# Keys transposed by a DMA, F and E turned first, and a fourth bank for the last block of an attention and MLP-mixer kernel

## The chip, the cores and the metric

One Trainium2 chip, one of its cores. The metric is the device time of one execution in microseconds (us), as the median of several runs.

## The reference

```python
# B=8 batches, H=8 heads, S=1024 positions, D=64 per head, all float32
k_proj = np.einsum('ks,bhsd->bhkd', E, k)        # E, F: 64 x 1024
v_proj = np.einsum('ks,bhsd->bhkd', F, v)
attn = softmax(np.matmul(q, k_proj.transpose(0, 1, 3, 2)) / 8)
x = np.matmul(attn, v_proj)                      # heads merged: B x 1024 x 512
u = x + (relu(x.T @ w_tok1) @ w_tok2).T          # token mixing, 256 wide, per batch
out = u + relu(u @ w_ch1) @ w_ch2                # channel mixing, 1536 wide
```

## The kernel before

TensorE does nearly everything. The channel mixing of a batch is done as two blocks (16 blocks in all). Each half of it is a two-by-two block product that takes seven products in place of eight, with sums and differences made by VectorE before and after. While blocks of batch b run, attention and token mixing of batch b+1 are woven in. A small list scheduler in Python decides the order of every engine's instructions ahead of time: each job has a due time (`prio`), and that order is then fixed in the program. In the traces an engine whose next instruction has to wait stands idle.

In the profile, L383 is the warm-up matmul on a zero tile, L411 the turning of E and F, L461 and L464 the projections E·k and F·v, L498 the small transposing matmuls of the projected keys, L803 the first half of a block, L898 its second half (`down_block`). In the kernel after, the same lines are L385, L413, L464 and L467, L513, L819 and L920; L575 is the matmul of the scores there (L559 before), L598 that of the attention with the projected values, whose result VectorE scales at L615 (`x_sb`), and L689 forms sums S from the transposed u (L673 before). The parts that the change touches:

```python
# the start
nc.vector.memset(vb, 0.0); nc.vector.memset(kT, 0.0)   # ... then, further down:
nc.vector.memset(zero, 0.0)                            # operand of the warm-up matmuls
for n, (src, dst) in enumerate(((EF[0], ET_sb), (EF[1], FT_sb))):   # E, then F
    ...                                                # 8 PE transposes each, one copy

# projected keys and values of a batch (batches 2 to 7: all 8 heads at once)
def kv_proj(b, h0, hn, due):
    ...                                # E k into rows 0-63 of a bank, F v into 64-127
    e = [copy -> kp[:, hs, 0, :], copy -> kp[:, hs, 1, :],       # keys twice
         copy -> vb[KP:, hs, 1, 0:D], copy -> vb[0:KP, hs, 0, 0:D]]   # 4 copies on ACT

def k_transpose(h0, hn, due):
    def mm():
        for h in range(hn):            # one 64-column matmul per head
            nc.tensor.matmul(view()[:, h, :], kp[:, h0 + h]..., ident[:KP, :KP], ...)
    ...                                # two ACT copies: the halves to the diagonal of kT

# the second half of a block: seven products, three banks
X_OF = {1: "x", 2: "x", 6: "y", 5: "y", 3: "y", 7: "z", 4: "z"}
def down_block(j):
    product(1, 0)
    act(... copy(out=view("y"), in_=view("x")) ...)     # y starts as a copy of product 1
    product(7, 1)
    product(6, 2)
    add_u(db, "db", "y", 1, 0)                          # db = y + u   (DVE)
    product(2, 3)
    add_u(o_of(0, 0), o_key(0, 0), "x", 0, 0)           # out00 = x + u
    product(5, 4)                                       # adds into y: must wait for db
    ... da = y + u ; out11 = z + da
    product(3, 5)                                       # adds into y: must wait for da
    add_u(o_of(0, 1), o_key(0, 1), "y", 0, 1)           # out01 = y + u
    store(0)                                            # 512 KB
    product(4, 6)
    ... out10 = z + db
    store(1)                                            # 512 KB
```

q and u are transposed by DMA, from the queue of SyncE (SP). Loads go out from POOL. The two "take turns" by explicit waits: k and v of batch b are loaded after the first transpose of u of batch b−2, the second transpose of u waits for the last of those loads, and the load of q waits for that transpose in turn.

The softmax here doesn't subtract the row's maximum and nothing guards it: scores larger than these inputs give would overflow.

## Time and profile before

| | before |
|---|---|
| time, median of 3 runs | 431.66 us (431.65 to 431.86) |
| profiled span | 429.8 us |
| TensorE busy | 97% of the span |
| first matmul, first projection of keys | 2.89 us, 9.94 us |
| first matmul of the last block, last matmul's start | 413.98 us, 425.13 us |

The page of the kernel before, its head: the span, each engine's busy time with its share and its number of instructions, the busy tenths of TensorE and of the DMA engines in 40 slices, and the engines' shares of the chain that ended last.

```profile
span 429.8 us, 9229 instructions
PE 415.9 (97%) x3727; PEld 336.2 (78%) x3756; DVE 321.9 (75%) x794; ACT 231.1 (54%) x428; POOL 66.3 (15%) x104
...
PE   7899999999999999999999999999999999999994
...
DMA  9999999996999785796939897498822303151122
...
PE 86%; DMA 6%; DVE 4%; ACT 2%; issue 1%; DVEq 0%
```

TensorE has work nearly all the time, in all slices but the first two and the last. So a gain has to come from matmuls that go away or from waits between them. The DMA engines are busy in the first half of the span, and have room in the second.

The four largest waits of TensorE of the kernel before from 1 to 73 us, each with whom it waited for, the total, how many and the longest:

```profile
PE ps L383 <- DVE zero L378: 2.9, 1, 2.9
PE ps L559 <- ACT kT L513: 0.9, 2, 0.6
PE ps L744 <- ACT uT L750: 0.4, 1, 0.4
PE ps L803 <- DVE S L673: 0.4, 1, 0.4
```

The first matmul waits 2.9 us for the zero tile.

The timeline of TensorE of the kernel before round one group of key transpositions (start, us, then engine, line, operation, shape, count):

```profile
176.16 0.60 PE L803 MATMUL ps<-S,wT 128*128 128x256 bf16 x4
176.69 0.41 PE L498 MATMUL ps<-ident,kp 64*128 64x64 bf16 x8
177.03 0.61 PE L803 MATMUL ps<-S,wT 128*128 128x256 bf16 x4
```

Ends of matmuls are modelled, so starts are what counts. Four matmuls of 256 columns take four slots of 0.109 us, up to 176.60; the next matmul after the group starts at 177.03. The group of eight costs PE 0.43 us, and there are six such groups in batches 2 to 7: 2.6 us.

The timeline of the last block of the kernel before (in brackets the idle time before a group and what ended it):

```profile
413.98 1.47 PE L898 MATMUL ps<-wc_sb,G 128*128 128x256 bf16 x12
...
419.63 0.68 DVE L931 TENSOR_TENSOR db<-ps,u 128x512 f32<-128x512 f32 x1
420.37 1.47 PE L898 MATMUL ps<-wc_sb,G 128*128 128x256 bf16 x12 [0.78 <-DVE db L931]
421.88 0.69 DVE L947 TENSOR_TENSOR da<-ps,u 128x512 f32<-128x512 f32 x1 [1.56 <-PE ps L898]
...
422.62 1.47 PE L898 MATMUL ps<-wc_sb,G 128*128 128x256 bf16 x12 [0.78 <-DVE da L947]
423.93 1.47 PE L898 MATMUL ps<-wT,G 128*128 128x256 bf16 x12
...
425.44 0.69 DVE L959 TENSOR_TENSOR o<-ps,db 128x512 f32<-128x512 f32 x1 [0.62 <-PE ps L898]
```

Products 5 (420.37) and 3 (422.62) each wait for VectorE to have read bank y. In every other block PE has other work to fill that time with; in the last there is none. By starts each wait costs 0.95 us. The Trainium skill ("PSUM — Partial Sum Buffer", the summary of rules for kernel authors) asks for just such a guard, by bank, and advises to read from a different bank than the one that matmuls write. The trace agrees with the cost side of it: the guard is seen as these two waits.

### The profile page before, as it was taken

To read this page: it belongs to the slowest core of one execution; us is meant where nothing else is said; L and a number is where in the kernel's file an instruction comes from. 1 tells how busy PE (TensorE), PEld (TensorE's weight loads), DVE (VectorE), ACT (ScalarE), POOL (GpSimd) and SP (SyncE) were. 2 spreads that over 40 slices of the span, in tenths; PEclk is the share of its full clock that TensorE was granted. 3 is DMA by queue.
4 is the path that set the end of the run, shared out by engine and by line. 5 is a ranking of instruction groups with operands and counts; after the bars stand their busy time and mean duration, and the time that the engine had idled before them with its cause. 6 is when DMAs were issued, how large, how long until landed. Compare 5 with 4: busy or idle time off the path is not lost.

```text
span 429.8 us, 9229 instructions
## 1 busy us (share of the span) xinstructions
PE 415.9 (97%) x3727; PEld 336.2 (78%) x3756; DVE 321.9 (75%) x794; ACT 231.1 (54%) x428; POOL 66.3 (15%) x104
## 2 busy tenths in 40 slices
PE   7899999999999999999999999999999999999994
PEld 3587886787878777787778878788778878888883
DVE  2369968797867878589577978679686887978573
ACT  1958895465457543863447644665438643444520
POOL 8443221030121110301111100211100000000000
PEclk9999999999999999999999999999999999999999
DMA  9999999996999785796939897498822303151122
GB/s 170 207 200 206 206 207 175 202 158 139 168 159 235 122 200 99 123 220 100 197 55 184 175 168 157 71 233 137 196 52 66 83 28 99 23 148 49 50 99 98
DMA packets 89513, 60.88 MB, mean 142 GB/s; under 512 B 55680, under 2 KB 84864, under 8 KB 89472
## 3 DMA queue, kind: packets, MB, share of 16 engines
q0 software_dynamic: 34944, 45.09, 53.2%
q1 hardware_dynamic: 54448, 14.95, 19.6%
q8 instruction: 29, 0.48, 0.4%
q10 hardware_dynamic: 80, 0.26, 0.3%
q14 instruction: 12, 0.10, 0.1%
HBM read 59.24 MB, written 16.78 MB: 177 GB/s over the span
## 4 chain that ended last, share of the span: by engine, by line
PE 86%; DMA 6%; DVE 4%; ACT 2%; issue 1%; DVEq 0%
PE ps L898 31%; PE ps L803 31%; PE ps L613 6%; PE ps L633 4%; DMA v_sb<-in_v_dram 3%; PE ps L582 3%; DMA uT<-u 3%; PE ps L461 3%; PE ps L559 3%; PE ps L383 1%; DVE u L644 1%; PE ps L691 1%; PE ps L718 1%; PE ps L543 1%; ACT qT L551 1%
## 5 line engine op out<-in xcount | busy, mean ns | idle before, releaser
L898 PEld LDWEIGHTS <-G 128*128 128x128 bf16 x1344 | 129.9, 98 | 25.1 <-issue 2.8
L898 PE MATMUL ps<-wc_sb,G 128*128 128x256 bf16 x768 | 104.1, 273 | 2.3 <-DVE da L947 1.5
L825 ACT ACTIVATE G<-ps 128x512 bf16<-128x512 f32 x96 | 56.7, 597 | 63.0 <-PE ps L803 62.8
L803 PEld LDWEIGHTS <-wc_sb 128*128 128x128 bf16 x768 | 73.2, 98 | 16.3 <-issue 2.4
L898 PE MATMUL ps<-wT,G 128*128 128x256 bf16 x576 | 78.2, 273 | 0.0
L803 PEld LDWEIGHTS <-wT 128*128 128x128 bf16 x576 | 55.2, 98 | 12.3 <-issue 1.2
L803 PE MATMUL ps<-S,wc_sb 128*128 128x256 bf16 x384 | 57.7, 273 | 0.3
L803 PE MATMUL ps<-uT,wc_sb 128*128 128x256 bf16 x384 | 57.8, 273 | 0.1
L803 PE MATMUL ps<-S,wT 128*128 128x256 bf16 x384 | 55.7, 273 | 0.4 <-DVE S L673 0.4
L784 DVE CUSTOM_DVE_ANT_0 g<-ps,ub 128x512 bf16<-128x512 f32 x48 | 32.8, 682 | 29.3 <-PE ps L803 29.3
L599 DVE TENSOR_TENSOR x_sb<-ps,rdn 128x256 bf16<-128x256 f32 x128 | 50.7, 415 | 0.9
L568 ACT ACTIVATE a<-ps 128x512 bf16<-128x512 f32 x64 | 37.8, 600 | 17.9 <-PE ps L559 17.2
L925 POOL DMA_DIRECT2D out_dram<-o x30 | 16.4, 545 | 192.8 <-DVE o L931 130.8
L831 ACT COPY ua<-ps 128x512 f32<-128x512 f32 x48 | 28.2, 587 | 32.9 <-PE ps L803 32.5
L644 DVE TENSOR_TENSOR u<-ps,x_sb 128x512 bf16<-128x512 f32 x56 | 37.6, 684 | 9.5 <-PE ps L633 5.4
L838 DVE TENSOR_TENSOR G<-G 128x512 bf16<-128x512 bf16 x96 | 39.8, 417 | 2.5
L784 DVE CUSTOM_DVE_ANT_0 G<-ps,ua 128x512 bf16<-128x512 f32 x48 | 32.8, 683 | 8.2 <-ACT ua L831 7.7
L844 ACT COPY ps<-ps 128x512 f32<-128x512 f32 x48 | 27.7, 577 | 17.1 <-DVE o L931 7.6
L831 ACT COPY ub<-ps 128x512 f32<-128x512 f32 x48 | 28.1, 586 | 13.6 <-PE ps L803 13.5
L594 DVE RECIPROCAL rdn<-ps 128x4 f32<-128x4 f32 x128 | 20.7, 173 | 18.0 <-PE ps L582 14.4
L582 PE MATMUL ps<-vb,a 128*128 128x130 bf16 x256 | 31.5, 220 | 0.4 <-DVE x_sb L599 0.3
L633 PE MATMUL ps<-hT_sb,wt_sb 128*128 128x512 bf16 x99 | 29.9, 379 | 0.4
(68 smaller groups left out, 496.2 us busy)
## 6 DMA issues: line engine op xcount, KB each, us to landing
out_dram<-o POOLq DMA_DIRECT2D x30, 512.0 KB, 5.6
k_sb<-in_k_dram POOLq DMA_DIRECT2D x14, 512.0 KB, 7.4
v_sb<-in_v_dram POOLq DMA_DIRECT2D x14, 512.0 KB, 11.8
q_sb<-in_q_dram POOLq DMA_DIRECT2D x14, 512.0 KB, 8.3
wc_sb<-in_moe_w_ch_dram POOLq DMA_DIRECT2D x6, 256.0 KB, 12.5
wc_sb<-in_moe_w_ch_dram POOLq DMA_DIRECT2D x4, 384.0 KB, 12.6
k_sb<-in_k_dram POOLq DMA_DIRECT2D x4, 256.0 KB, 6.8
v_sb<-in_v_dram POOLq DMA_DIRECT2D x4, 256.0 KB, 7.3
```

The source lines that it names most:

```text
L568: lambda: nc.scalar.activation(out=a_t[h % 4], in_=bank(bk), func=ACT.Exp, scale=scale),
L582: nc.tensor.matmul(view()[:, 2 * jj : 2 * jj + 2].rearrange("p c d -> p (c d)"), a_t[h % 4][:, j * P : (j + 1) * P], vb[:, h].rearrange("k ...
L599: lambda: nc.vector.tensor_tensor(out=x_sb[:, 4 * half : 4 * half + 4, h * D : (h + 1) * D], in0=view()[:, :, 0:D], in1=rdn[:, :, None].to ...
L633: nc.tensor.matmul(bank(bk), wt2_sb[:, t, si::NSI], hT_sb[:, t, :], start=(t == 0), stop=(t == TC - 1),)
L644: lambda: nc.vector.tensor_add(out=u_t[b % 2][:, si, :], in0=bank(bk), in1=x_sb[:, si, :]),
L784: nc.vector._custom_dve(TENSOR_ADD_SAT, out=out, in0=in0, in1=in1, s0=FMAX, s1=0.0)
L803: nc.tensor.matmul(t[:, c, :], w1_of(n, dd, 2 * m + c), a_of(j, n, dd), start=(n in (1, 7) and c == 0 and dd == 0), stop=(c == 1 and dd == 1),
L825: lambda: nc.scalar.activation(out=G[:, n, cs], in_=view(src), func=ACT.Relu),
L831: 512, lambda: nc.scalar.copy(out=dst, in_=view("y")), writes=[(name, s % 2)],
L838: 512, lambda: f(out=G[:, n, cs], in0=in0, in1=in1), ps=False, reads=deps,
L844: 512, lambda: nc.scalar.copy(out=view("y"), in_=view("x")), takes=[bk["y"]],
L898: nc.tensor.matmul(view(X_OF[n])[:, t, :], G[:, G_OF[n], cc, t * P : (t + 1) * P], w2_of(n, cc), start=(n in (1, 7) and t == 0 and cc == 0 ...
```

## The change

Three independent parts, each meant to take something off TensorE's path:

1. The start: the zero tile is written first, F is turned before E, and fewer warm-up matmuls are put ahead of the turning, so PE begins earlier.
2. The keys of batches 2 to 7: the projection puts the keys as blocks on the diagonal of a tile `kb`, and a single DMA transposes `kb` to `kT`. Eight small matmuls and two ACT copies per batch go. The projection is asked for 12 us earlier (`EARLY`), so that the DMA has time to land.
3. The last block: products 5 and 3 go to a fourth bank w, y is left at product 1 plus 6, and VectorE puts the two together, with eight adds in the block in place of six. The order of products is fixed as 1, 7, 6, 5, 2, 3, 4, and the output goes out in four stores of 256 KB in place of two of 512 KB.

```diff
+EARLY = 12.0
@@ the start
+    zero = tile_of([P, P], BF16, "zero")
+    nc.vector.memset(zero, 0.0)
     nc.vector.memset(vb, 0.0)
     nc.vector.memset(kT, 0.0)
+    nc.vector.memset(kb, 0.0)
...
-    zero = tile_of([P, P], BF16, "zero")
-    nc.vector.memset(zero, 0.0)
...
-    for n, (src, dst) in enumerate(((EF[0], ET_sb), (EF[1], FT_sb))):
+    for n, (src, dst) in enumerate(((EF[1], FT_sb), (EF[0], ET_sb))):
...
-            for _ in range(int((j.start - idle - 0.3) / 0.216) if spare is not None else 0):
+            for _ in range(int((j.start - idle - 0.3) / 0.216) if spare is not None and j.prio > -100 else 0):
                 blank(spare)
@@ the keys
+        if block:
+            k_to = [kb[i * KP : (i + 1) * KP, hs, i, :] for i in range(2)]
+        else:
+            k_to = [kp[:, hk, i, :] for i in range(2)]
...
+    def k_transpose_dma():
+        sp(
+            2.5,
+            lambda: nc.sync.dma_start_transpose(
+                out=kT.rearrange("p h c k -> p h (c k)"), in_=kb.rearrange("p h r d -> p (h r d)")
             ),
...
-            unit(1.9 * hn / H, lambda t, i=i: kv_proj(b, i * hn, hn, t))
-            unit(0.9 * hn / H, lambda t, i=i: k_transpose(i * hn, hn, t))
+            if b == 1:
+                unit(1.9 * hn / H, lambda t, i=i: kv_proj(b, i * hn, hn, t))
+                unit(0.9 * hn / H, lambda t, i=i: k_transpose(i * hn, hn, t))
+            else:
+                unit(1.9, lambda t: kv_proj(b, 0, H, t - EARLY, True))
+                unit(0.0, lambda t: k_transpose_dma())
@@ the last block
+        last = j == NSB - 1
+        where, opens = X_OF, (1, 7)
+        if last:
+            bk["w"] = Bank("F")
+            where, opens = {**X_OF, 5: "w", 3: "w"}, (1, 7, 5)
...
+        p5 = product(5, 3)
+        follow(p5[0], p6[1])
+        add_u(da, "da", "y", 1, 1)
+        da_w = add(da, "da", "w", da, "da")
+        follow(product(2, 4)[0], p5[1])
+        c22 = add(o_of(1, 1), o_key(1, 1), "z", da, "da")
+        store(1, (1,))
+        follow(add_u(dc, ("ub", 0), "y", 0, 1), da_w)
+        follow(add_u(db, "db", "y", 1, 0), c22)
+        follow(add_u(o_of(0, 0), o_key(0, 0), "x", 0, 0), c22)
+        product(3, 5)
+        store(0, (0,))
+        add(o_of(0, 1), o_key(0, 1), "w", dc, ("ub", 0))
+        store(0, (1,))
+        product(4, 6)
+        add(o_of(1, 0), o_key(1, 0), "z", db, "db")
+        store(1, (0,))
```

(Left out are the names of dependencies and the smaller key tile `kp` that batches 0 and 1 keep.)

More of the change, by code (lines that the diff above doesn't have):

```diff
@@ L266 @@
     kT = tile_of([P, H, 2, KP], BF16, "kT")
-    kp = tile_of([KP, H, 2, D], BF16, "kp")
+    kp = tile_of([KP, H // 2, 2, D], BF16, "kp")
+    kb = tile_of([P, H, 2, D], BF16, "kb")
     ET_sb = tile_of([P, NSI, KP], BF16, "ET_sb")
@@ L374, in due_d @@
         return TU * j + 23.8 + 1.76 * i
-    zero = tile_of([P, P], BF16, "zero")
-    nc.vector.memset(zero, 0.0)
-    pin()
     def blank(b):
@@ L413, in take @@
         def take(n=n, dst=dst, view=view):
-            (nc.scalar.copy if n else nc.vector.tensor_copy)(out=dst, in_=view())
+            (nc.vector.tensor_copy if n else nc.scalar.copy)(out=dst, in_=view())
         pl.add("PE", 1.6, 1.6, turn, reads=["ident"], takes=[b], prio=-150)
-        (act if n else dve)(512, take, writes=["ET", "FT"][n : n + 1], uses=[b], prio=-150)
+        (dve if n else act)(512, take, writes=["FT", "ET"][n : n + 1], uses=[b], prio=-150)
     def combine(T, b11, b12, b21, b22, cols, name, n, reads):
@@ L447, with kv_proj @@
     stream = ["S"]
-    def kv_proj(b, h0, hn, due):
+    def kv_proj(b, h0, hn, due, block=False):
         hs = slice(h0, h0 + hn)
+        hk = slice(h0 % (H // 2), h0 % (H // 2) + hn)
         heads = range(h0, h0 + hn)
@@ L474, in kv_proj, with copy @@
         )
-        e = [
-            lambda: nc.scalar.copy(out=kp[:, hs, 0, :], in_=view()[0:KP, 0:hn]),
-            lambda: nc.scalar.copy(out=kp[:, hs, 1, :], in_=view()[0:KP, 0:hn]),
-            lambda: nc.scalar.copy(
-                out=vb[KP : 2 * KP, hs, 1, 0:D], in_=view()[KP : 2 * KP, 0:hn]
-            ),
-            lambda: nc.scalar.copy(out=vb[0:KP, hs, 0, 0:D], in_=view()[KP : 2 * KP, 0:hn]),
-        ]
-        act(cols, e[0], writes=[("kp", 0, h) for h in heads], uses=[bk])
-        act(cols, e[1], writes=[("kp", 1, h) for h in heads], uses=[bk])
-        act(cols, e[2], writes=[("vb", 1, h) for h in heads], uses=[bk])
-        act(cols, e[3], writes=[("vb", 0, h) for h in heads], uses=[bk])
+        src = [lambda: view()[0:KP, 0:hn], lambda: view()[KP : 2 * KP, 0:hn]]
+        if block:
+            k_to = [kb[i * KP : (i + 1) * KP, hs, i, :] for i in range(2)]
+        else:
+            k_to = [kp[:, hk, i, :] for i in range(2)]
+        v_to = [vb[i * KP : (i + 1) * KP, hs, i, 0:D] for i in range(2)]
+        def copy(to, n):
+            return lambda: nc.scalar.copy(out=to, in_=src[n]())
+        for i in range(2):
+            act(cols, copy(k_to[i], 0), writes=[("kb" if block else "kp", i, h if block else h % (H // 2)) for h in heads], uses=[bk])
+        for i in (1, 0):
+            act(cols, copy(v_to[i], 1), writes=[("vb", i, h) for h in heads], uses=[bk])
+    def k_transpose_dma():
[3 more added lines that the diff above has]
+                out=kT.rearrange("p h c k -> p h (c k)"), in_=kb.rearrange("p h r d -> p (h r d)")
+            ),
+            reads=[("kb", i, h) for i in range(2) for h in range(H)],
+            writes=[("kT", i, h) for i in range(2) for h in range(H)], prio=None,
+        )
     def k_transpose(h0, hn, due):
@@ L498, in mm @@
                 nc.tensor.matmul(
-                    view()[:, h, :], kp[:, h0 + h].rearrange("k r d -> k (r d)"),
+                    view()[:, h, :], kp[:, h0 % (H // 2) + h].rearrange("k r d -> k (r d)"),
                     ident[:KP, :KP], start=True, stop=True,
@@ L503, in k_transpose @@
         pe(
-            hn, 64, mm, reads=[("kp", i, h) for i in range(2) for h in heads], takes=[bk], prio=due,
+            hn, 64, mm, reads=[("kp", i, h % (H // 2)) for i in range(2) for h in heads], takes=[bk],
+            prio=due,
             after=[("kT", i, h) for i in range(2) for h in heads],
@@ L898, in mm @@
                 nc.tensor.matmul(
-                    view(X_OF[n])[:, t, :], G[:, G_OF[n], cc, t * P : (t + 1) * P], w2_of(n, cc),
-                    start=(n in (1, 7) and t == 0 and cc == 0), stop=(cc == C2 - 1),
+                    view(where[n])[:, t, :], G[:, G_OF[n], cc, t * P : (t + 1) * P], w2_of(n, cc),
+                    start=(n in opens and t == 0 and cc == 0), stop=(cc == C2 - 1),
                     skip_group_check=True,
@@ L908, in product @@
                 w = [("W2", c, n) for c in range(2)]
-            bb = bk[X_OF[n]]
+            bb = bk[where[n]]
+            jobs = []
             for t in range(2):
-                first = n in (1, 7) and t == 0
-                pe(
+                first = n in opens and t == 0
+                jobs.append(pe(
                     C2, 256, lambda t=t: mm(n, t),
@@ L916, in product, with store @@
                     prio=due_d(j, 2 * i + t),
-                )
-        queue = nc.gpsimd if j < NSB - 1 else nc.sync
-        def store(sh):
+                ))
+            return jobs
+        def store(sh, halves=(0, 1)):
             rows = slice(i * NJ + 2 * sh, i * NJ + 2 * sh + 2)
-            sp(
-                1.5, lambda: queue.dma_start(out=out_v[b, :, rows, :], in_=o_t[os[sh]]),
-                reads=[o_key(sh, 0), o_key(sh, 1)], prio=None,
+            cs = slice(halves[0] * DH, (halves[-1] + 1) * DH)
+            queue = nc.sync if last else nc.gpsimd
+            sp(
+                1.5, lambda: queue.dma_start(out=out_v[b, :, rows, cs], in_=o_t[os[sh]][:, :, cs]),
+                reads=[o_key(sh, dh) for dh in halves], prio=None,
             ).early = True
         def add_u(dst, key, src, sh, dh):
-            dve(
+            return dve(
                 512, lambda: nc.vector.tensor_add(out=dst, in0=view(src), in1=u_of(sh, dh)),
@@ L940, in down_block @@
         product(7, 1)
-        product(6, 2)
+        p6 = product(6, 2)
+        if last:
+            return finish(p6, product, add_u, store, bk, view, o_of, o_key)
         add_u(db, "db", "y", 1, 0)
@@ L962, in down_block, with finish, add, follow @@
         store(1)
+    def finish(p6, product, add_u, store, bk, view, o_of, o_key):
+        dc = ub_t[0]
+        def add(dst, key, src, part, part_key):
+            return dve(
+                512, lambda: nc.vector.tensor_add(out=dst, in0=view(src), in1=part),
+                reads=[part_key], writes=[key], uses=[bk[src]],
+            )
+        def follow(j, other):
+            j.deps.add(other)
+        p5 = product(5, 3)
[15 more added lines that the diff above has]
+        store(1, (0,))
     for hp in range(HP):
```

## The prediction

> **What bounds it now.** TensorE: the busy table gives PE 97% of a 429.8 us span. By matmul starts, it is full: 256-column matmuls follow each other every 109 ns, as the Trainium skill ("TensorE: Matmul & The Clock Gate", Part 1: N / 2.4 GHz + about 2.5 ns) has it. After 71 us the only PE waits over 0.3 us are 0.88 us at 126.7 and 0.51 at 145.9 (DVE held up by a DMA transpose of u), and two of 0.95 us in the last block (420.4, 422.6: for DVE's read of the bank that PE adds into).
> Before 73 us loads are the limit, landing back to back. Two gate PE: v of batch 1 (lands 47.42, used 47.47), of batch 2 (70.27, used 70.64).
>
> **The change, costed.**
> 1. Start. The zero tile is ready 1.6 us earlier, two warm-up matmuls go, F is turned first. PE gets 1.5-2 us ahead, but its order up to the gates is the same and loads are no faster: it will wait at the 47.4 gate. Worth 0.3 us.
> 2. Keys by DMA in batches 2 to 7. Away: 6 groups of 8 small matmuls (0.43 us of PE each, 2.6 in all) and 12 ACT copies (0.5 us each, off the path). Added: 6 DMA transposes of half the size of q's and u's. Three full ones in a row (115.9 to 125.7) took 3.3 us each, so I estimate 1.6-2 us of DMA time each. The Trainium skill ("Trainium Kernel Development and Optimization", Key Constraints) says that DMAs of all queues interleave on the same 16 engines; here these are 84-99% busy from 83 to 169 us. There transposes and loads form one chain (u's transpose gates the next loads), and two of the added ones go into it: q of batch 3 comes some 3 us later, while the new order wants batch 3's first scores 5 us of PE work earlier. The 1.6 us of waits become 2 to 3: a loss of about 1. From batch 4 on DMA has some 5 us to spare per batch, and 0.43 us is pure gain.
> 3. Last block. Products 5 and 3 get their own bank. 84 matmuls worth 9.16 us took 11.26: -2.1. DVE then has eight adds of 0.7 us behind 5.2 us of PE: its last add ends 0.4 us later after the last matmul. Half the last store: -0.3.
>
> **Sum.** 431.7 - 0.3 - 2.6 + 1.0 - 2.0 = about 427.7. I predict **427.6 us**, 80% range **425.3 to 430.2**. Chances: faster by over 2% 3%, within 2% 96%, slower 1%.
>
> **What would show it.** (1) First matmul near 1.3 us, first key projection near 8; v of batch 1 still landing near 47.4, with a PE wait of 1.5-2 us before it. (2) No small transposing matmuls after batch 1; kT transposes of 2-4 us to landing; u's transposes of batches 1 and 2 landing 2-4 us later; a wait at batch 3's first scores, near 123 us. (3) No PE wait over 0.2 us in the last block, DVE back to back; last store landing 2.3 us after issue.
>
> **What would make it wrong.** kT transposes much slower next to loads, or holding the queue before u's, so that PE waits several us (over 430); or those waits vanish because the new order leaves more time before each use, or the earlier start is kept (under 425.3).

## The result

| | before | after |
|---|---|---|
| time, median of 4 runs each of the same rounds | 431.76 us | 427.91 us (427.5 to 428.23) |
| ratio after to before | | 0.991 (95%: 0.9893 to 0.9928) |
| profiled span | 429.8 us | 426.3 us |
| first projection of keys, batch 0 | 9.94 us | 7.61 us |
| projection of keys, batch 2 | 70.64 us | 70.64 us |
| first matmul of the last block | 413.98 us | 412.45 us |
| last matmul's start | 425.13 us | 421.51 us |
| from there to the end of the last add | 1.00 us | 1.00 us |
| from the last matmul's start to the end of the span | 4.69 us | 4.79 us |

A ratio is the mean time of one kernel's fast runs over that of the other's of the same rounds, so it is not quite the ratio of the medians quoted. The change makes the kernel 0.9% faster, within the 2% that counts as the same, and the forecast of 427.6 us is 0.3 us off. A later repeat of the changed kernel as it is, in other rounds (`after_b` below), gave 0.9939, a gain smaller by 0.3%, so the total is known to about a microsecond.

The page of the kernel after, the same lines:

```profile
span 426.3 us, 9187 instructions
PE 415.2 (97%) x3706; PEld 334.8 (79%) x3706; DVE 323.3 (76%) x797; ACT 225.5 (53%) x416; POOL 66.3 (16%) x104
...
PE   8899999999999999999999999998999999999995
...
DMA  9999999989899799997969874896850602250223
...
PE 81%; DMA 11%; DVE 5%; issue 1%; POOL 1%; POOLq 0%; DVEq 0%; SPq 0%
```

Busy shares hardly move and do not show the gain: PE's busy time went from 415.9 to 415.2 us, while the span lost 3.5. What tells more is the chain that ended last, where the DMA's share went from 6% to 11%. (The counts of matmuls are not to be compared: some records are missing in each trace.)

**The start: an earlier beginning, no gain.** The four largest waits of TensorE of the kernel after, 1 to 73 us:

```profile
PE ps L385 <- DVE zero L289: 1.0, 1, 1.0
PE ps L559 <- DMA q_sb<-in_q_dram: 0.9, 2, 0.7
PE ps L707 <- DMA wt_sb<-in_moe_w_tok_dram: 0.7, 1, 0.7
PE ps L467 <- DMA v_sb<-in_v_dram: 0.6, 1, 0.6
```

PE begins 1.9 us earlier, and its first projection of keys 2.3 us earlier, at 7.61 us. That is just when its last operands are there: the copy of the turned E ended at 7.56, and v landed at 7.59. From there on the loads of batch 0 mostly land 1.2 to 1.3 us apart and PE waits for one after the other, by starts 0.87 us at 8.96, 0.74 at 11.47, 0.31 at 12.77, 0.34 at 16.60, 0.84 at 20.07 and 0.29 at 23.91, of which there was none before. The lead is gone well before 47 us: there PE starts its projection of batch 1 at 47.35 without waiting, since v had landed at 47.11. (Before, PE started at 47.11 and waited for v until 47.47.) At 70.64 both are level.

**The keys: 2.6 us of matmuls gone, about half of it given back.** From 70.64 us, where both stand alike, to the first matmul of the last block, the kernel after is 1.53 us shorter. The six groups of small matmuls are gone (−2.6), but waits of over 0.15 us rose from 1.58 us in all (0.88 + 0.51 + 0.19) to 2.95 (0.20 + 0.31 + 0.58 + 0.19 + 1.28 + 0.17 + 0.22), which is +1.37. That leaves −1.23, and the remaining −0.3 must lie in pauses under 0.15 us. (This is one profile of each kernel; more of them are compared below.) The two places that matter, in the timeline of the kernel after:

```profile
124.15 0.38 PE L575 MATMUL ps<-qT,kT 128*128 128x512 bf16 x1 [0.41 <-DMA qT<-q_sb]
...
290.08 0.43 DVE L689 TENSOR_TENSOR S<-uT 128x512 bf16<-128x512 bf16 x1 [1.87 <-DMA uT<-u]
...
290.89 0.22 PE L598 MATMUL ps<-vb,a 128*128 128x130 bf16 x1 [1.12 <-DVE x_sb L615]
```

The first line is batch 3's first scores matmul, which waits for the transposition of q (0.58 us by starts): the place that the prediction named. The other two are one event: VectorE can't form its sums S until the transposed u has landed, stands for 1.87 us, and what it does next (`x_sb`) is what PE then waits for. PE's line names VectorE; the cause is the DMA one step back. The chain of waits of the kernel after shows how long these transfers took (start, us):

```profile
109.34 8.73 DMA q_sb<-in_q_dram
118.14 5.97 DMA qT<-q_sb
282.77 7.29 DMA uT<-u
```

and the medians from issue to landing of each kernel's transfers show what was normal, here before,

```profile
out_dram<-o SPq DMA_DIRECT2D x2, 512.0 KB, 2.6
uT<-u SPq DMA_TRANSPOSE x14, 4.7
qT<-q_sb SPq DMA_TRANSPOSE x12, 5.9
```

and here after:

```profile
out_dram<-o SPq DMA_DIRECT2D x4, 256.0 KB, 2.6
uT<-u SPq DMA_TRANSPOSE x14, 5.6
qT<-q_sb SPq DMA_TRANSPOSE x12, 5.1
kT<-kb SPq DMA_TRANSPOSE x6, 3.3
```

A key transposition lands in 3.0 to 3.6 us four times out of six; the one of batch 3, issued among loads of q, took 8.9 us (109.71 to 118.61). The u transposition of 282.77 took 7.29 us; a store of 512 KB had been issued 0.03 us before it. The Trainium skill ("Trainium Kernel Development and Optimization", Key Constraints) says that the DMAs of all queues run on the same 16 engines and interleave. The trace agrees, 8.9 us beside loads against 3.0.

**The last block: two waits gone.** The timeline of the last block of the kernel after:

```profile
412.45 1.47 PE L920 MATMUL ps<-wc_sb,G 128*128 128x256 bf16 x12
...
413.76 2.78 PE L920 MATMUL ps<-wT,G 128*128 128x256 bf16 x24
...
416.38 4.09 PE L920 MATMUL ps<-wc_sb,G 128*128 128x256 bf16 x36
...
417.89 0.69 DVE L995 TENSOR_TENSOR da<-ps,da 128x512 f32<-128x512 f32 x1 [0.55 <-PE ps L920]
418.50 0.68 DVE L955 TENSOR_TENSOR ub<-ps,u 128x512 f32<-128x512 f32 x1
419.09 0.68 DVE L995 TENSOR_TENSOR o<-ps,da 128x512 f32<-128x512 f32 x1
...
420.31 1.47 PE L920 MATMUL ps<-wT,G 128*128 128x256 bf16 x12
...
421.82 0.69 DVE L995 TENSOR_TENSOR o<-ps,db 128x512 f32<-128x512 f32 x1 [0.25 <-PE ps L920]
```

PE runs its 84 matmuls without a bracket, from 412.45 to 421.51: 9.06 us, against 11.15 before, −2.09. VectorE's adds from 417.89 to 420.89 start 0.60 us after each other, though each record lasts 0.68 or 0.69, and its last add still waits 0.25 us for PE. So PE, not VectorE, sets the end, and the time from the last matmul to the last add is 1.00 us in both kernels. The last store, half as large, was issued at 422.54 and landed at 425.25 (2.71 us); before, at 426.16 and 428.78 (2.62 us).

The account of the span: start 0.00, keys −1.53, last block −2.09, behind it +0.10, in all −3.52 us; 429.8 less 426.3 is 3.5.

### The profile page after: what moved, and what is told of

It is laid out like the page before. It is cut to its first block, busy times and chain, and to the rows that moved or that the text cites. A ratio compares the mean times of both kernels' runs of the same rounds, so it can differ in the third digit from the quotient of the medians.

```text
span 426.3 us, 9187 instructions
## 1 busy us (share of the span) xinstructions
PE 415.2 (97%) x3706; PEld 334.8 (79%) x3706; DVE 323.3 (76%) x797; ACT 225.5 (53%) x416; POOL 66.3 (16%) x104
## 4 chain that ended last, share of the span: by engine, by line
PE 81%; DMA 11%; DVE 5%; issue 1%; POOL 1%; POOLq 0%; DVEq 0%; SPq 0%
PE ps L920 32%; PE ps L819 30%; DMA q_sb<-in_q_dram 5%; PE ps L629 5%; PE ps L649 5%; DMA uT<-u 3%; PE ps L575 3%; PE ps L598 3%; PE ps L464 3%; DMA v_sb<-in_v_dram 1%; DMA qT<-q_sb 1%; DVE u L746 1%; DVE x_sb L615 1%; DVE S L689 1%; PE ps L559 1%
## 5 line engine op out<-in xcount | busy, mean ns | idle before, releaser
L841 ACT ACTIVATE G<-ps 128x512 bf16<-128x512 f32 x96 | 57.1, 597 | 69.2 <-PE ps L819 69.2
L649 PE MATMUL ps<-hT_sb,wt_sb 128*128 128x512 bf16 x112 | 32.7, 379 | 0.0
```

The lines of the kernel that those rows point to most:

```text
L649: nc.tensor.matmul(bank(bk), wt2_sb[:, t, si::NSI], hT_sb[:, t, :], start=(t == 0), stop=(t == TC - 1),)
L841: lambda: nc.scalar.activation(out=G[:, n, cs], in_=view(src), func=ACT.Relu),
```

## The experiments

My theory after the result: the start gains nothing (the loads decide), the keys gain about one microsecond because the DMA path gives half back, and the last block gains two. The rivals: the start does gain and something else loses; the keys gain the full 2.6 us in an undisturbed run and the wait at 291 us is an accident; or the last block's gain is the new order alone and the bank is not needed. Twelve runs of ten kernels were made, in three groups, each group on one chip with its own runs of the kernel before. The changed kernel itself ran again in the third group alone; in the first two, a variant is compared with it through their ratios to the kernel before. All results were right.

| kernel | median us | its before | ratio, 95% |
|---|---|---|---|
| a_start: only part 1 | 431.45 | 431.83 | 0.9987, 0.9972 to 1.0002 |
| a_keys: only part 2 | 431.21 | 431.83 | 0.9984, 0.9965 to 1.0003 |
| a_last: only part 3 | 429.51 | 431.83 | 0.9940, 0.9923 to 0.9957 |
| a_keys4: all three, keys by DMA from batch 4 | 427.49 | 431.83 | 0.9895, 0.9877 to 0.9914 |
| early0: EARLY = 0 | 454.05 | 431.56 | 1.0516, 1.0486 to 1.0545 |
| kt_twice: key transposition issued twice | 430.84, of 3 fast runs | 431.56 | 1.0001, 0.9967 to 1.0035 |
| last_order: before, last block's order alone | 430.46 | 431.56 | 0.9971, 0.9950 to 0.9993 |
| u_first: u's second transposition not held | 429.30 | 431.56 | 0.9949, 0.9923 to 0.9975 |
| after_b: the changed kernel again | 428.89 | 431.77 | 0.9939, 0.9921 to 0.9958 |
| keys4_b: a_keys4 again | 428.18 | 431.77 | 0.9926, 0.9891 to 0.9961 |
| keys4_tail: and two adds on GpSimd | 428.19 | 431.77 | 0.9918, 0.9902 to 0.9933 |
| kt_twice_b: kt_twice, one look | 430.24 | 431.77 | none |

### The three parts alone

`a_start` undoes parts 2 and 3, `a_keys` parts 1 and 3, `a_last` parts 1 and 2. The edits are the diff above taken back; at their core:

```diff
 a_start, a_last:
-            if b == 1:
+            if True:                       # keys of all batches by PE again
 a_start, a_keys:
-        last = j == NSB - 1
+        last = False                       # the last block as the others, its stores on SP
 a_keys, a_last: zero tile late, E before F, no limit on the warm-up matmuls
```

> Only the start of the change (zero tile first, F turned first, no warm-up matmuls in front of the turns), the rest as before. Theory (PE runs ahead but waits for loads until v of batch 2 lands near 70 us): first key projection about 2 us earlier, key projection of batch 2 within 0.4 us of before's 70.64, time 0.2 to 0.5 us under before, about 431.4. Rival (the earlier start is kept to the end): 1.5 to 2 us under before, about 430.

> Only the keys by DMA (batches 2 to 7, projection asked for 12 us earlier), start and last block as before. Theory (2.6 us of PE work go, but new waits on the DMA chain and on DVE held up by it give 1 to 1.5 back): 1.0 to 1.6 us under before, about 430.4. Rival (the added transposes cost nothing on the path): 2.6 us under before, about 429.1.

> Only the last block (fourth bank, new order, stores in halves); every instruction before it is as in before. Theory: the block's 84 matmuls start within 9.1 us instead of 11.2, and the last add and store give 0.1 back: 1.8 to 2.1 us under before, about 429.7. Rival (DVE, with one add more, takes most of it back): under 1 us.

Measured: `a_start` 0.13% faster and `a_keys` 0.16%, both with an interval that just includes no gain; `a_last` 0.60%. The rivals of the first two (gains of 1.5 to 2 us, and of 2.6 us) lie outside the intervals, which end at 1.2 and 1.5 us. By the ratios `a_keys` gained 0.7 us, less than the 1.0 to 1.6 forecast, and `a_last` 2.6 us, more than its 1.8 to 2.1; both forecasts lie partly within the intervals. The three add up to 0.89%, and the whole change was 0.90% in its own rounds (0.61% in the repeat): within noise of some 0.3% the parts do not disturb each other. In the profile of `a_start` the keys of batch 2 are projected at 70.53 us, against 70.64: nothing of the earlier start is left there. In that of `a_keys` the first matmul of the last block starts at 412.85, which is 1.13 us earlier than before, although six groups worth 2.6 us are gone. Its waits are the same as in the whole change: 0.93 us by starts at batch 3's first scores (for the transposition of q), and 1.10 us at 291.3 with two small ones after it. In the profile of `a_last` the last block takes 9.06 us, as in the whole change.

The other profiles allow a check on the keys. From the projection of batch 2's keys to the first matmul of the last block, the four with the order of before (`before`, `a_start`, `a_last`, `last_order`) took 342.41 to 343.39 us, with waits of 0.61 to 1.58 us; the three with the order of after (`after`, `after_b`, `a_keys`) took 341.81 to 342.11 us, with waits of 2.95 to 3.24 us. The means differ by 1.1 us, so the 1.53 of the first pair is at the upper end, and more waits are seen each time.

What follows: more than half of the gain comes from the last block. The rival that the keys gain 2.6 us undisturbed is ruled out, and the wait near 291 us is not an accident of one profile.

### Does the DMA path give the gain back in batches 2 and 3?

In `a_keys4` the keys of batches 2 and 3, in the stretch where the DMA engines are busiest, go by PE again, and only batches 4 to 7 by DMA. In `u_first` the wait that holds u's second transposition behind the loads of k and v is dropped, and the loads are held until u has been transposed. `kt_twice` issues each key transposition twice, to double its DMA time with the same order of all else. (In its trace the second of a pair is issued only when the first has landed, 0.02 us after it, so the queue of SP is held as well.)

```diff
 a_keys4, keys4_b (with kp of all 8 heads again):
-            if b == 1:
+            if b < 4:
 u_first:
-        last = load_group(b, "kv", turned_u.get((b - 2, 0)))
-        if (b - 2, 1) in turned_u:
-            tie(turned_u[b - 2, 1], last)
+        load_group(b, "kv", turned_u.get((b - 2, 1)))
 kt_twice, kt_twice_b:
-            lambda: nc.sync.dma_start_transpose(
+            lambda: [nc.sync.dma_start_transpose(
                 out=kT.rearrange(...), in_=kb.rearrange(...)
-            ),
+            ) for _ in range(2)],
```

> The changed kernel with keys by DMA only from batch 4 on; batches 2 and 3, where transposes and loads form one serial DMA chain, turn them on PE as before. Theory (the two transposes there cost about as much in waits as the 0.86 us of PE work that they save): within 0.5 us of the changed kernel, 427.4 to 428.4, with the PE waits near 88 and 124 us gone and u's transposes of batches 1 and 2 landing 1 to 2 us earlier. Rival (those two transposes are free): 0.9 us slower than the changed kernel, about 428.8.

> The changed kernel with the turns of loads and transposes changed: both transposes of u first, then the loads of k and v, then those of q (before: first half of u, k and v, second half of u, q). Theory (the waits that are left, 0.6 us at 124 and 1.7 at 291, come from a half of u that lands when DVE already stands at the sums made of it): DVE's waits for the second halves of u go, 1 to 2.5 us under the changed kernel, about 426. Rival (the DMA time is the same, so what u gains k, v and q lose): PE waits at the key projection of batch 3 or its first scores instead, no gain or slower.

> The changed kernel with each of the six key transposes issued twice in a row (the same data again, all else in the same order). Theory (a key transpose costs 1.3 to 2 us of the DMA chain, and those of batches 2 and 3 go straight into the landing of batch 3's queries): the PE wait at batch 3's first scores grows from 0.6 to 2.5 to 4 us, u's first transposes of batches 4 to 7 come 1 to 2 us later and eat most of DVE's slack there; 2 to 4 us slower than the changed kernel, about 431. Rival (the transposes run beside the loads for nothing): under 0.5 us slower.

Measured: `a_keys4` was the fastest of all, 427.49 us (0.9895). In its profile PE has no wait over 0.3 us after 70 us, and the last block begins at 410.98 us: 3.00 earlier than before, from four groups (4 × 0.43 = 1.72) and the 1.58 us of waits of before, less 0.3. That is one execution, the fastest of its five (426.37 us): in the profile of its repeat `keys4_b` PE waits 0.73 us at 126.9, where the kernel before waited 0.88, and in that of `keys4_tail`, which has the same order up to the last block, 0.50 at 106.5, 0.63 at 126.9 and 0.78 at 291.3. So keeping these two groups on PE takes the wait near 124 us away, but brings back the one near 126.7 in some executions, and it does not by itself remove the one near 291.

`u_first` gave a profile with neither wait (0.69 us at 189.5 is its longest one), in the fastest of its runs, 426.17 us. But its timed runs spread from 427.71 to 430.5 and its ratio of 0.9949 is no better than the changed kernel's. The one profile shows the best case and not the usual one; no gain is shown.

`kt_twice` had one execution of 1525.23 us, the profiled one. It is counted as a slow run and not used. Its trace shows that TensorE alone was slow: matmuls of 256 columns mostly started 0.420 us apart, from the beginning to the end, against 0.109 elsewhere, while a typical ScalarE instruction (L841) took 597 ns as in the kernel after. The trace holds no record of the clock, so the cause is open. The other three gave 433.32, 430.84 and 430.77 us. By its ratio of 1.0001 it is 2.7 to 3.9 us slower than the changed kernel at 0.9939 or 0.9910, as forecast, though not measured in the same rounds.

> kt_twice once more for its profile alone (the first one fell in an execution of 1525 us[...]). Theory: queries of batch 3 land 2 to 4 us later than in the changed kernel, and PE waits 2.5 to 4 us at batch 3's first scores; time about 431. Rival: waits as in the changed kernel.

Measured: 430.24 us in the single look, whose state can't be told, 1.35 us over the median of the changed kernel in the same group, but still within the range of its runs (428.10 to 430.78), so the time alone shows nothing. The timeline of `kt_twice_b` at batch 3's first scores:

```profile
126.73 0.38 PE L575 MATMUL ps<-qT,kT 128*128 128x512 bf16 x1 [1.76 <-DMA qT<-q_sb]
```

With the key transposition doubled the wait for q's transposition here rose from 0.58 to 1.92 us by starts, less than the 2.5 to 4 forecast, and two new waits for the two halves of u of batch 1 appeared (0.82 at 89.8 and 0.66 at 110.0). These halves landed at 89.73 and 109.94 us, against 86.66 and 108.00 in the kernel after, and q's transposition at 126.68 against 124.10. This is the prediction's chain shown directly: the key transpositions of batches 2 and 3 push u's and q's transpositions back, and PE waits at the place that was named.

### What EARLY is for

```diff
-EARLY = 12.0
+EARLY = 0.0
```

> The changed kernel with the projection of keys not asked for 12 us earlier (the plan is made anew, so its order changes). Theory (the 12 us are there to hide copies and DMA transpose, about 6 us from the projection to the landing of kT, before the first scores): the plan puts the scores later, and PE waits for kT in several batches, 1 to 4 us slower than the changed kernel. Rival (the scores had time enough anyway): within 0.5 us.

Measured: 454.05 us, 5.2% slower than before. The waits of TensorE of `early0`, the largest:

```profile
PE ps L575 <- DMA kT<-kb: 18.2, 4, 5.6
```

Four times PE stands for 4 to 6 us at the first scores of a batch (starts at 136.4, 191.4, 248.4 and 303.8 us), for the keys' transposition and nothing else. 18.2 us of the 26.1 that its profiled span is longer than the changed kernel's are in these four waits (18.8 by starts). There is a second cost. The granted clock of TensorE in the 40 slices, which is 9 throughout in the kernels before and after:

```profile
PEclk9999999999997999889999899988999999999999
```

Around the end of each of the four waits the granted clock was 0.50, and it stayed there until 3.0 to 5.7 us after the wait, with matmuls of 256 columns starting 0.213 us apart in place of 0.109. By starts these stretches cost some 10 us more; against that, the waits of 2.95 us of the kernel after are nearly all gone. None of the waits of up to 1.9 us after 70 us in the other fast profiles shows such a dip. A DMA in place of 0.43 us of PE pays here only because the operand is asked for 12 us ahead.

### The last block: the order or the bank?

`last_order` is the kernel before with the order of products in the last block fixed as 1, 7, 6, 2, 5, 3, 4, and with three banks.

```diff
+        def chain(js, other):
+            if j == NSB - 1:
+                js[0].deps.add(other[1])
+            return js
-        product(2, 3)
+        p2 = chain(product(2, 3), p6)
-        product(5, 4)
+        p5 = chain(product(5, 4), p2)
         ...                                # likewise 3 after 5, and 4 after 3
```

> The kernel before with only the order of the last block's products forced to 1,7,6,2,5,3,4 (the planner had pulled 2 ahead of 6); no fourth bank, stores whole. Theory (PE has a product to do while DVE reads the y bank after 6, but none while it reads it after 5): one of the two waits of 0.95 us goes and the other stays, 0.9 to 1.2 us under before; so the fourth bank is worth the other half. Rival (the fourth bank alone makes the gain): both waits stay, no gain.

Measured: 0.29% faster than before, where the whole part 3 is 0.60%. Its last block takes 10.00 us from the first to the last matmul's start (before 11.15, after 9.06), and a single wait is left in its timeline, for the read of `da` ahead of product 3:

```profile
421.43 1.47 PE L921 MATMUL ps<-wc_sb,G 128*128 128x256 bf16 x12 [0.78 <-DVE da L978]
```

So 1.15 us of the 2.09 come from order alone, since product 2 then covers VectorE's read ahead of product 5, and the remaining 0.94 came with the fourth bank. The rival, that the bank alone makes the gain, is refuted, and the other one, that the order alone does, holds for about half. Whether a finer interleaving than by whole products could hide the last wait without a fourth bank was not tried.

### Can both be beaten?

`after_b`, `keys4_b` and `keys4_tail` ran on one chip in five rounds. `keys4_tail` is `a_keys4` with two of VectorE's eight last adds moved to GpSimd, on a copy of bank y, to test whether VectorE's adds set the end.

```diff
+        yc = ua_t[0]
+        act(512, lambda: nc.scalar.copy(out=yc, in_=view("y")), ...)
+        for dst, key, sh, dh in ((dc, ("ub", 0), 0, 1), (db, "db", 1, 0)):
+            pl.add("POOL", 1.0, 1.2, lambda ...: nc.gpsimd.tensor_add(out=dst, in0=yc, in1=u_of(sh, dh)), ...)
-        follow(add_u(dc, ("ub", 0), "y", 0, 1), da_w)
-        follow(add_u(db, "db", "y", 1, 0), c22)
```

> The changed kernel once more, unchanged, as the measure for the two that follow on the same chip. Expected as before: 0.991 of the kernel before, about 427.9, and PE waits of 0.3 to 1.5 us that move from run to run near 88, 124 and 291 us.

> The changed kernel with keys by DMA only from batch 4 on (as a_keys4), beside the changed kernel on the same chip. Theory (the key transposes of batches 2 and 3 cost as much in waits as they save on PE): 0 to 1 us under the changed kernel. Rival (they are free there too): 0.9 us slower than it.

> keys4_b with two of the last block's eight adds taken from DVE: ACT copies the y bank once, POOL adds u to the copy. Theory (the last add ends 1.0 us after the last matmul's start plus its length because DVE is back to back, where 0.9 is the least): the last add ends about 0.4 us sooner after the last matmul, 0.4 us under keys4_b. Rival (POOL's adds are slow, or ACT and POOL come too late for DVE): DVE waits for POOL, no gain or slower.

Measured: means of 429.11, 428.54 and 428.23 us. The two variants lie 0.6 and 0.9 us under the changed kernel, but the intervals of their ratios overlap with its own, and one run of `keys4_b` took 432.37. So no version is shown to beat the changed kernel; `a_keys4` and its repeat point the same way both times, but what is shown is only that keys by DMA in batches 2 and 3 bring no gain that can be seen. The timeline of the last adds in `keys4_tail`:

```profile
421.03 0.69 DVE L995 TENSOR_TENSOR o<-ps,ub 128x512 f32<-128x512 f32 x1 [0.68 <-PE ps L920]
...
422.34 0.69 DVE L995 TENSOR_TENSOR o<-ps,db 128x512 f32<-128x512 f32 x1 [0.62 <-PE ps L920]
```

VectorE now stands idle for 0.68 and 0.62 us ahead of its last two adds, and the last add still ends 1.07 us after the last matmul's start (1.00 in the changed kernel). The 0.4 us forecast did not come. Fewer adds on VectorE bought nothing: it was not what set the end.

The wait near 291 us, for which the second half of u of batch 5 must land, was 1.28 us by starts in the profile of the changed kernel, 1.77 in its repeat, 1.10 in `a_keys`, 0.78 in `keys4_tail`, 0.75 in `kt_twice_b`, 0.18 in `keys4_b`, and not over 0.3 in `a_keys4`. It moves from run to run with the same program, since the landing of that transposition moves by microseconds (4.75 to 7.29 us after its issue, over these seven profiles) and the fixed order leaves little room for it. Why it is issued so close to a store at just this batch, the loads of k of batch 7 show, before and after:

```profile
273.13 0.75 POOL L320 DMA_DIRECT2D k_sb<-in_k_dram  x1 [14.49 <-PE ps L464]
268.24 0.75 POOL L326 DMA_DIRECT2D k_sb<-in_k_dram  x1 [11.89 <-DMA uT<-u]
```

Before, these loads waited for the projection of batch 6 (from 270.92 us), which reads the buffer. With `EARLY` that projection is over by then (from 257.08 us), and the loads go out as soon as the first half of u has landed. The last of them lands at 282.63 us in place of 288.25, and the second transposition of u, tied to it, is issued at 282.77, just behind the store of 282.74 (282.92 before). Over the seven profiles it took 5.74 to 7.29 us when issued 0.03 to 0.71 us after that store, and 4.75 to 5.52 us at 1.26 to 1.43 us. This fits a collision with the store, but no run moves the store alone.

## Why the prediction was right

The total was right, 427.6 against 427.91 us, and so was the weight of the parts, within what can be told apart:

| part | predicted | account of the two profiles | alone, from the ratio |
|---|---|---|---|
| start | −0.3 | 0.0 | −0.6 (0.0013 × 431.8), may be none |
| keys | −1.6 (−2.6 + 1.0) | −1.5 (−1.1 over seven profiles) | −0.7, may be none |
| last block and tail | −2.0 (−2.1 + 0.4 − 0.3) | −2.0 (−2.1 + 0.1) | −2.6 |

Point by point:

- **"84 matmuls worth 9.16 us took 11.26: −2.1."** Right: they took 9.06 from first to last start, and −2.09. `last_order` adds that over half of it is the order. The slot of 0.109 us per matmul, which the prediction took from the Trainium skill and the trace, holds in the block to the end.
- **"6 groups … 0.43 us of PE each" and "The 1.6 us of waits become 2 to 3: a loss of about 1."** Right in sum: 1.58 became 2.95, +1.37. The named wait at batch 3's first scores exists (0.58 us), and `kt_twice_b` shows its mechanism. But the share was wrong. The delays of u's transpositions in batches 1 and 2 were about 1 to 2 us, not 2 to 4, and q's was 3.8, and 1.67 of the 2.95 us lie near 291 us.
- **"From batch 4 on DMA has some 5 us to spare per batch, and 0.43 us is pure gain."** This step failed in batch 5. On average the spare time is there; but the transposition of u took 7.29 us just then, issued beside a store, and spare time on average doesn't help a transfer that is late at the moment that an engine needs it. What I had not asked is what else `EARLY` moves (the loads behind the projection, and with them that transposition), and how much time the new order leaves between the issue of each transposition and its first use.
- **"It will wait at the 47.4 gate."** The worth of the start was right (0.3 predicted, none in the profile, 0.1% with an interval down to none alone), the place was wrong. The lead is lost between 9 and 24 us, to one load of batch 0 after another, and at 47.35 PE starts without waiting. The rule behind it (loads set the pace until 70 us) is what matters and it held; the gate that I picked is only the last one of a row.
- **"DVE then has eight adds of 0.7 us behind 5.2 us of PE: its last add ends 0.4 us later."** Wrong: mis-sized from the length of a record. Back to back they start every 0.60 us, so VectorE keeps up, and the term measured 0.00. The Trainium skill ("VectorE: DVE Perf Modes", The DRAIN you can't avoid) says that the next instruction waits until the pipe is empty, and that one that isn't held may start earlier. The trace agrees with the second: 0.60 us from start to start at 0.68 us of record. I should have read starts, as I did for PE.
- **"Half the last store: −0.3."** Wrong: 2.62 us at 512 KB and 2.71 at 256 KB (2.39 for the first of the four stores). I scaled the whole time with the size. The Trainium skill ("DMA: Bandwidth & Descriptors", Latency and other measured facts) speaks of a fixed cost of about 2 us, most of it the round trip to memory, and the trace agrees with a time that hardly depends on the size. The two errors (0.4 us forecast and 0.0 measured, −0.3 forecast and +0.1 measured) cancel, which is luck and not insight.
- **(1) to (3), what would show it.** First matmul 1.00 (1.3 forecast), first projection 7.61 (8), no small transposes after batch 1, and no PE wait over 0.2 us in the last block: as forecast. Four of six key transpositions landed within the forecast 2 to 4 us, but two, with 4.94 and 8.9, did not. VectorE was "back to back" from its second add to its last but one only. The last store landed 2.71 us after its issue, not 2.3.

## What to carry to other kernels

When a piece of work moves from a full engine to a DMA, ask for it well ahead (here 12 us, without which the kernel lost 5%, a good part of it to the halved clock after each long wait), and then look not at its own landing alone but at what it pushes back in the same queue and engines, and at what the earlier request lets start sooner: here about half of the gain was lost to waits for other transpositions. An average of idle DMA time is no promise; compare, use by use, the time from issue to first need with the slowest landing seen. And in the last block, where nothing else fills a wait, first reorder the products, then spend a free bank, and cost back-to-back vector work by the distance of starts.

## What the Trainium skill lacked or had wrong

- "DMA: Bandwidth & Descriptors" (Rules for kernel authors) says that "a transpose next to ordinary DMAs needs nothing". That is about correct data, and all runs agree. In time it does cost something, for which I found no figure on any page: the same key transposition took 3.0 us and, issued among loads of q, 8.9; u's took 4.2 at the least, and 7.29 when issued 0.03 us after a 512 KB store.
- "VectorE: DVE Perf Modes" (The three transpose paths) compares the paths for a single block of 128x128 only. Here eight such blocks in one DMA took 3.0 to 3.6 us to land when little else ran, against 0.43 us of TensorE time for the eight small matmuls that they replaced (which also took two ACT copies).
- "TensorE: Matmul & The Clock Gate" (Part 1, Seeing it yourself) mentions a clock gate seen stuck at a quarter for over 50 us, without a cause. No page that I found tells of a whole execution like the one of 1525 us (one of four of a kernel), in which matmuls of 256 columns started 0.420 us apart in place of 0.109; that it was the clock is not shown, since this trace has no record of it.
